# Attention and two wide layers on one core: where the 256-key bias slabs and the first weight unit stand in the start

## Chip, core and metric

The kernel runs on one core of a Trainium2 chip. The metric is the device time in microseconds (us). Three timed runs of the kernel before gave 657.86, 659.28 and 660.02 us, a median of 659.28 us. The profiled execution took 659.89 us in all, and the span from its first to its last instruction is 657.6 us; all times inside the trace are counted from the start of that span.

The engines are called as in the profile: PE (matrix multiply, with PEld for its weight loads), DVE (vector), ACT (scalar and activation), POOL (GpSimd), SP (here only the queue that issues transfers).

## What is computed

Attention with a local window, a few global keys and a distance bias, and behind it two wide layers with other nonlinearities:

```python
scores = scale * q @ k.T                       # B=2, H=8, S=768, D=64
keep   = is_global | is_local                  # 8 global keys, 96 local ones
bias   = -slopes[h] * dist                     # dist is the distance, n_local for far global keys
scores = where(keep, scores + bias, -1e9)
x = softmax(scores) @ v                        # as 1536 tokens x 512
h = x @ w_in;   x = (relu(h) + log1p(exp(-|h|))) @ w_out      # 512 -> 2048 -> 512
h = x @ w_in2;  x = (h * clip(h + 3, 0, 6) / 6) @ w_out2
```

## The kernel before

**Attention by quads.** Each batch of 768 rows is cut into 6 blocks of 128 rows, so that there are 12 blocks. A quad is one block and four heads, so there are 24 of them, two to a block, counted 0 to 23. A block sees its own keys and those of the block before it (256 keys), and the first block of a batch sees only its own (128 keys). For a quad, `att_s` makes the scores on PE (L481). Per head, DVE then adds the bias slab and takes the row's minimum of the negated scores (L487, called a minima instruction here), and ACT does the exponential with its row sum (L492). DVE adds a small constant to the row sums and takes the reciprocal (L377, L378, "rs"), and POOL scales the rows by it (L380). `att_t` transposes the scaled rows on PE (L513), ACT copies the result out (L515, "pT"), and `att_v` multiplies by the values (L531). Behind the second quad of a block ACT and DVE split the block's result into a high and a low part (L538, L539).

**Bias slabs.** The tile `bias` holds for each of the 8 heads three slabs of 128 keys. The slab for the own block of a first block (index 2) is made on ACT (L446, eight instructions). The slabs for 256 keys (indices 0 and 1) are made on DVE by `bias_of` (L449), one instruction for a head, from the mask tile `far` (L441 to L444). Quads 0 and 1 belong to the first block and need only L446. Quad 2 is the first that needs L449.

**Weights by units.** The weights come as 64-bit words in units of 512 KB. A unit is loaded (L121, on SP), its absolute value is taken on ACT (L140) and clamped on POOL (L143). DVE rebuilds its bits in three steps (L144, L147, L148), POOL rounds it to the high part (L103), and DVE subtracts to get the low part (L153). `weight_step(m)` puts m units into the program, with the loads of up to five units ahead of the one at hand. Both layers are made of such units; the first multiplication of the first layer (`hf`, from L201) needs units 0 and 1, the second one (`accf`) needs units 4 and 5.

**The start.** The lead at L616 to L628 makes 12 multiplications of zeros (`warm`, L614), then for p = 0 to 4 the scores of all quads up to p + 2, the values, more `warm`, the transposes and the units of `LEAD_UNITS`. Just ahead of quad 2's scores it makes one unit and all eight 256-key slabs. Behind the lead, `layers.run` mixes the remaining quads into the first layer: two quads into the first `hf` item, one into every later half.

**What sets the order.** PE's order is the program's, by `keep_in_program_order`. On the other engines a scheduler of the framework places the instructions, with the bias slabs held in program order. Every engine runs its own instructions strictly in the order in which they stand.

Of the kernel before, what the change touches and what calls it, by code (L numbers as in the profile page):

```python
# [12 lines left out]
ALU = mybir.AluOpType  # L13
# [4 lines left out]
B, H, S, D = 2, 8, 768, 64  # L18
# [14 lines left out]
LEAD_UNITS = (2, 1, 1, 1, 1)  # L33
# [6 lines left out]
SCALE = 0.125  # L40
# [342 lines left out]
def fast_path(tc, ident, nf, counts, q, k, qt, kt, v, weights, out, flag):  # L383


    with ExitStack() as ctx, ExitStack() as actx:
# [58 lines left out]
        for h in range(H):  # L445
            nc.scalar.mul(bias[:, h, 2, :], far[:, 2, :], -SLOPES[h] / SCALE)  # L446

        def bias_of(h):
            tc.keep_in_program_order(nc.vector.tensor_scalar(  # L449
                out=bias[:, h, 0:2, :], in0=far[:, 0:2, :], scalar1=-SLOPES[h] / SCALE, scalar2=None, op0=ALU.mult  # L450
            ))

        pms, pTs = {}, {}
        s_tags = [(ps_s, f"s{j}") for j in range(2)]
# [1 line left out]
        def att_s(k):  # L456

            n, e = divmod(k, KC // 2)
            i, slot = n % NB, n % 3
            if e == 0:  # L460
                if n + 1 < B * NB:
                    load_block(n + 1)
                load_values(n)
                if i == 0:
                    nc.vector.tensor_copy(gk, kT[:, :, slot, 0:MAX_GLOBAL])
            before = (n - 1) % 3
            w = P if i == 0 else 2 * P
            nsl = w // P
            mo = 2 if i == 0 else 0
            step = before - slot  # L470
            end = slot + nsl * step
            ks = slice(slot, min(end, 3) if end >= 0 else None, step)
            two = layers.acc_tags if k < LEAD and k % 2 else s_tags
            ps = [layers.bank(t, f"s{k}_{j}", (P, 2, 2, P)) for j, t in enumerate(two)]
            pm = ap_m.tile([P, 4, 2 * P], F32, tag="pm", name=f"pm{k}")
            nm = ap_m.tile([P, 4], F32, tag="nm", name=f"nm{k}")
            sm = ap_m.tile([P, 4], F32, tag="sm", name=f"sm{k}")
            for a in range(2):
                for j in range(2):
                    hp = slice(j * D, (j + 1) * D)  # L480
                    layers.ordered(lambda: nc.tensor.matmul(  # L481
                        ps[j][:, a, 0:nsl, :], lhsT=qT[n][hp, 2 * e + a, :], rhs=kT[hp, 2 * e + a, ks, :],
                        start=True, stop=True,
                    ))
            for z in range(4):
                pmz = pm[:, z, 0:w]
                nc.vector.tensor_tensor_reduce(  # L487
                    out=pmz, in0=ps[z % 2][:, z // 2, 0:nsl, :].rearrange("p s t -> p (s t)"),
                    in1=bias[:, 4 * e + z, mo:mo + nsl, :].rearrange("p s t -> p (s t)"),
                    scale=-SCALE, scalar=3.0e38, op0=ALU.add, op1=ALU.min, accum_out=nm[:, z:z + 1],  # L490
                )
                nc.scalar.activation(pmz, pmz, AF.Exp, bias=nm[:, z:z + 1], scale=-1.0, accum_out=sm[:, z:z + 1])  # L492
            rs = ap_m.tile([P, 4], F32, tag="rs", name=f"rs{k}")
            softmax_rows(nc, sm, rs, [pm[:, z, 0:w] for z in range(4)])
            if e == KC // 2 - 1 and 1 <= i < NB - 1:
                nc.vector.tensor_copy(kT[:, :, slot, 0:MAX_GLOBAL], gk)
            pms[k] = pm
# [118 lines left out]
        warm_up(WARM)  # L616
        for p in range(LEAD):
            while step["s"] < min(p + AHEAD, quads):
                if step["s"] == 2:
                    layers.weight_step(1)  # L620
                    for h in range(H):
                        bias_of(h)
                att_step("s")
            att_step("v", p - V_LAG + 1)
            warm_up(FILL[p])
            for _ in range(2):
                att_step("t")
            layers.weight_step(LEAD_UNITS[p] - (p == 0))  # L628
        layers.run(Att, check_step)


# [176 lines left out]
```

## Time and profile before

| quantity | value |
|---|---|
| median of three timed runs | 659.28 us |
| profiled execution, in all | 659.89 us |
| its span | 657.6 us |
| PE busy | 628.1 us (96% of the span) |
| DVE, ACT, POOL busy | 429.8, 375.4, 148.5 us |
| mean granted PE clock | 0.988 of full speed |

The share of busy time alone does not tell where time is lost: PE is nearly always busy behind the first 75 us, and has its holes ahead of them. So the table of stretches, the list of waits and the order of time of the first 75 us are what is to be read here.

### The profile page before, as it was taken

The numbers are of one execution on the slowest core, as the hardware profiler recorded it, in microseconds if no ns is written. First come the engines' busy times: TensorE is split into PE (matmuls) and PEld (weight loads), VectorE is DVE, ScalarE is ACT, GpSimd is POOL, SyncE is SP. The second block draws the span as 40 slices with busy tenths as digits, with TensorE's granted clock in tenths as the row PEclk, the third lists the DMA queues.
The fourth block names the chain that finished last, engine by engine and source line by source line (L and its number), as shares of the span: only waits on it lengthen the run. The fifth ranks groups of instructions, "written<-read, shape, count | busy, mean of one in ns | idle before, by whom it ended". The sixth has DMA issues, their size and how long they took to land.

```text
span 657.6 us, 9611 instructions
## 1 busy us (share of the span) xinstructions
PE 628.1 (96%) x3481; PEld 514.6 (78%) x3481; DVE 429.8 (65%) x902; ACT 375.4 (57%) x786; POOL 148.5 (23%) x192
## 2 busy tenths in 40 slices
PE   8587998999999999999999999999999999999995
PEld 4366887889999888877788888888877888888874
DVE  5897568654789999999998995225832333424242
ACT  5577778775587977867687852325675222212220
POOL 3575454531024132625200420000100000000000
PEclk9698999999999999999999999999999999999999
DMA  8452331101035233433311132000473000001011
GB/s 281 168 201 87 116 97 53 37 21 70 33 98 160 96 129 104 136 113 112 129 48 52 46 129 96 1 1 32 118 219 81 0 1 0 1 1 64 1 65 69
DMA packets 24937, 53.67 MB, mean 82 GB/s; under 512 B 2480, under 2 KB 8880, under 8 KB 24880
## 3 DMA queue, kind: packets, MB, share of 16 engines
q1 hardware_dynamic: 24880, 52.96, 24.8%
q8 instruction: 29, 0.48, 0.3%
q14 instruction: 28, 0.23, 0.1%
HBM read 49.81 MB, written 3.15 MB: 81 GB/s over the span
## 4 chain that ended last, share of the span: by engine, by line
PE 62%; DVE 19%; ACT 6%; DMA 4%; POOL 4%; issue 3%; SPq 0%; ACTq 0%; POOLq 0%; DVEq 0%
PE acc L201 22%; PE h L201 22%; PE accf L201 6%; PE hf L201 5%; DMA chk<-in_q 3%; DVE wa L147 2%; DVE wa L148 2%; POOL pm L380 2%; DVE w L153 2%; ACT pm L492 2%; PE ptp L513 2%; DVE pm L487 2%; PE s L481 2%; POOL wa L143 1%; DVE gl L193 1%
## 5 line engine op out<-in xcount | busy, mean ns | idle before, releaser
L201 PE MATMUL h<-xsh,w 128*128 128x512 f32 x624 | 170.3, 396 | 0.4 <-DVE t L187 0.4
L201 PEld LDWEIGHTS h<-xsh,w 128*128 128x128 f32 x624 | 116.7, 188 | 29.5 <-DVE t L187 1.6
L143 POOL TENSOR_SCALAR wa<-wa 128x512 f32<-128x512 f32 x56 | 76.3, 1368 | 240.2 <-ACT wa L140 239.9
L201 PE MATMUL acc<-w,gh 128*128 128x512 f32 x384 | 120.6, 395 | 0.0
L191 DVE SCALAR_TENSOR_TENSOR t<-t,h 128x512 f32<-128x512 f32 x48 | 32.9, 686 | 96.7 <-ACT t L190 96.7
L190 ACT ACTIVATE t<-h,three 128x512 f32<-128x512 f32 x48 | 33.0, 687 | 105.2 <-PE h L201 105.1
L201 PE MATMUL h<-xsl,w 128*128 128x512 f32 x312 | 87.8, 396 | 0.0
L193 DVE TENSOR_TENSOR gl<-t,gh 128x512 fp32r<-128x512 f32 x78 | 55.2, 708 | 47.3 <-ACT gh L192 47.0
L201 PEld LDWEIGHTS acc<-w,gh 128*128 128x128 f32 x384 | 72.0, 188 | 17.4
L201 PE MATMUL acc<-gh,w 128*128 128x512 f32 x240 | 78.9, 396 | 0.3 <-DVE part L297 0.2
L201 PE MATMUL acc<-w,gl 128*128 128x512 f32 x192 | 76.3, 397 | 0.8 <-ACT part L303 0.4
L192 ACT CAST gh<-t 128x512 fp32r<-128x512 f32 x78 | 48.3, 619 | 50.3 <-PE acc L201 24.3
L201 PEld LDWEIGHTS h<-xsl,w 128*128 128x128 f32 x312 | 58.5, 188 | 14.1
L380 POOL TENSOR_SCALAR pm<-pm,rs 128x256 f32<-128x256 f32 (+1 forms) x96 | 51.0, 549 | 44.5 <-DVE rs L378 33.2
L201 PE MATMUL accf<-ghf,w 128*128 128x256 f32 x288 | 59.6, 291 | 0.6 <-ACT ghf L192 0.6
L492 ACT ACTIVATE pm<-pm,nm 128x256 f32<-128x256 f32 (+1 forms) x96 | 46.0, 480 | 16.5 <-DVE nm L487 16.3
L201 PEld LDWEIGHTS acc<-gh,w 128*128 128x128 f32 x240 | 44.9, 188 | 11.9 <-DVE part L297 0.6
L201 PEld LDWEIGHTS accf<-ghf,w 128*128 128x128 f32 x288 | 47.3, 191 | 2.2 <-issue 1.2
L201 PE MATMUL acc<-gl,w 128*128 128x512 f32 x120 | 47.5, 396 | 0.0
L153 DVE TENSOR_TENSOR w<-wa,w 128x512 fp32r<-128x512 f32 x56 | 38.9, 696 | 9.2 <-ACT w L105 8.3
L201 PE MATMUL hf<-xsh,w 128*128 128x256 f32 x288 | 44.8, 286 | 0.0
L201 PEld LDWEIGHTS acc<-w,gl 128*128 128x128 f32 x192 | 36.0, 188 | 11.0 <-DVE gl L193 1.7
(105 smaller groups left out, 989.2 us busy)
## 6 DMA issues: line engine op xcount, KB each, us to landing
raw<-in_w2i SPq DMA_DIRECT2D x16, 512.0 KB, 3.3
raw<-in_w2o SPq DMA_DIRECT2D x16, 512.0 KB, 3.3
raw<-in_w1i SPq DMA_DIRECT2D x14, 512.0 KB, 3.6
raw<-in_w1o SPq DMA_DIRECT2D x12, 512.0 KB, 3.3
V<-in_v SPq DMA_DIRECT2D x12, 256.0 KB, 2.9
chk<-in_q SPq DMA_DIRECT2D x12, 256.0 KB, 3.3
chk<-in_k SPq DMA_DIRECT2D x12, 256.0 KB, 2.8
out_x<-part SPq DMA_DIRECT2D x12, 256.0 KB, 2.1
```

The costliest lines, as they stand in the source:

```text
L143: nc.gpsimd.tensor_scalar(out=a, in0=a, scalar1=W_HI, scalar2=W_LO, op0=ALU.min, op1=ALU.max)
L147: nc.vector.scalar_tensor_tensor(out=ai, in0=hi, scalar=-2 ** 30, in1=ai, op0=ALU.bitwise_and, op1=ALU.bitwise_or)
L148: nc.vector.scalar_tensor_tensor(out=ai, in0=lo, scalar=29, in1=ai, op0=ALU.logical_shift_right, op1=ALU.bitwise_or)
L153: nc.vector.tensor_tensor(out=wl, in0=a, in1=r32(wh), op=ALU.subtract)
L190: nc.scalar.activation(t1, hf, AF.Relu, bias=self.three[:, 0:1])
L191: nc.vector.scalar_tensor_tensor(out=t3, in0=t1, scalar=6.0, in1=hf, op0=ALU.min, op1=ALU.mult)
L192: nc.scalar.copy(gh, t3)
L193: nc.vector.tensor_tensor(out=gl, in0=t3, in1=r32(gh), op=ALU.subtract)
L201: return self.nc.tensor.matmul(out, lhsT=a, rhs=b, start=start and z == 0, stop=stop and z == len(seq) - 1, **kw)
L380: nc.gpsimd.tensor_scalar(out=t, in0=t, scalar1=rs[:, j:j + 1], scalar2=0.0, op0=ALU.mult, op1=ALU.add)
L481: layers.ordered(lambda: nc.tensor.matmul(ps[j][:, a, 0:nsl, :], lhsT=qT[n][hp, 2 * e + a, :], rhs=kT[hp, 2 * e + a, ks, :], start=True, s ...
L492: nc.scalar.activation(pmz, pmz, AF.Exp, bias=nm[:, z:z + 1], scale=-1.0, accum_out=sm[:, z:z + 1])
```

## The change

The eight slabs are no longer made ahead of quad 2. Four of them (heads 0 to 3) stand directly behind the masks, ahead of quad 0's minima; the other four stand inside `att_s` of quad 0, behind its minima. The one unit of weights that stood ahead of quad 2 goes, and p = 0 makes two units where it made one, so that the lead has six units as before.

```diff
-        def bias_of(h):
-            tc.keep_in_program_order(nc.vector.tensor_scalar(
-                out=bias[:, h, 0:2, :], in0=far[:, 0:2, :], scalar1=-SLOPES[h] / SCALE, scalar2=None, op0=ALU.mult
-            ))
+        def bias_of(hs):
+            for h in hs:
+                tc.keep_in_program_order(nc.vector.tensor_scalar(
+                    out=bias[:, h, 0:2, :], in0=far[:, 0:2, :], scalar1=-SLOPES[h] / SCALE, scalar2=None, op0=ALU.mult
+                ))
+
+        bias_of(range(H // 2))
...
                 nc.scalar.activation(pmz, pmz, AF.Exp, bias=nm[:, z:z + 1], scale=-1.0, accum_out=sm[:, z:z + 1])
+            if k == 0:
+                bias_of(range(H // 2, H))
...
             while step["s"] < min(p + AHEAD, quads):
-                if step["s"] == 2:
-                    layers.weight_step(1)
-                    for h in range(H):
-                        bias_of(h)
                 att_step("s")
...
-            layers.weight_step(LEAD_UNITS[p] - (p == 0))
+            layers.weight_step(LEAD_UNITS[p])
```

PE's order is the same in both. On the other engines the order differs from quad 0 to about quad 12 and is the same from there to the end of the path that is executed. Three places follow; the line numbers of the changed kernel are up to five higher (L490 is L487 of before, L450 is L449, L495 is L492, L520 is L515).

On DVE, behind the minima of quads 0 and 1. Before (`part_90` is the scratch tile of weight units 0 to 3, `w_0` to `w_3` are converted weights, `pm_269` is quad 2):

```order
L496 COPY kT<-gk 128x4x32
L144 TENSOR_SCALAR part_90<-part_90 128x512
L147 SCALAR_TENSOR_TENSOR part_90<-part_89,part_90 128x512
L148 SCALAR_TENSOR_TENSOR part_90<-part_89,part_90 128x512
...
L147 SCALAR_TENSOR_TENSOR part_90<-raw_0_237,part_90 128x512
L153 TENSOR_TENSOR w_0_244<-part_90,w_0_243 128x512
L449 TENSOR_SCALAR bias<-far 128x256 x8
L153 TENSOR_TENSOR w_1_309<-part_90,w_1_308 128x512
L148 SCALAR_TENSOR_TENSOR part_90<-raw_0_237,part_90 128x512
L487 ISA pm_269,nm_270<-s_0_267,bias 128x256
```

DVE, the same place and what leads up to it, in the changed kernel (`pm_193`, `pm_221`, `pm_250`, `pm_321` are quads 0 to 3, `rs_212` belongs to quad 0, `rs_336` to quad 3):

```order
L450 TENSOR_SCALAR bias<-far 128x256 x4
L490 ISA pm_193,nm_194<-s_0_191,bias 128x128
...
L450 TENSOR_SCALAR bias<-far 128x256 x4
L490 ISA pm_221,nm_222<-s_0_219,bias 128x128
...
L377 TENSOR_SCALAR rs_212<-sm_195 128x4
L490 ISA pm_250,nm_251<-s_0_248,bias 128x256
...
L378 RECIPROCAL rs_212<-rs_212 128x4
...
L490 ISA pm_321,nm_322<-s_0_319,bias 128x256
...
L378 RECIPROCAL rs_336<-rs_336 128x4
L144 TENSOR_SCALAR part_90<-part_90 128x512
```

The slabs and the minima of quads 2 and 3 moved ahead of the first unit's DVE work, which was most of three units ahead of quad 2 and is now mixed with the minima of quads 4 to 8.

On ACT, from quad 1's exponentials on. Before:

```order
L492 ACTIVATE pm_213,sm_215<-pm_213,nm_214 128x128 x4
L140 ACTIVATE part_90<-part_89 128x512
L515 COPY pT_0_298<-ptp_0_297 128x2x128
L515 COPY pT_1_303<-ptp_1_302 128x2x128
L140 ACTIVATE part_90<-part_89 128x512
L515 COPY pT_0_354<-ptp_0_353 128x2x128
L515 COPY pT_1_359<-ptp_1_358 128x2x128
L140 ACTIVATE part_90<-raw_0_237 128x512
L492 ACTIVATE pm_269,sm_271<-pm_269,nm_270 128x256 x4
```

ACT, the same place in the changed kernel (`pm_250` is quad 2, `pm_321` quad 3):

```order
L495 ACTIVATE pm_221,sm_223<-pm_221,nm_222 128x128 x4
L495 ACTIVATE pm_250,sm_252<-pm_250,nm_251 128x256 x4
L520 COPY pT_0_279<-ptp_0_278 128x2x128
L520 COPY pT_1_284<-ptp_1_283 128x2x128
L140 ACTIVATE part_90<-part_89 128x512 x2
L495 ACTIVATE pm_321,sm_323<-pm_321,nm_322 128x256 x4
```

Quad 2's exponentials moved ahead of the first units' L140; quad 3's stand behind the first two of them.

On DVE, ahead of the first `glf`, the low part that the first `accf` multiplies by. Before (`pm_814` is quad 10):

```order
L188 TENSOR_TENSOR t3f_699<-t3f_699,t2f_700 128x512
L153 TENSOR_TENSOR w_2_367<-part_90,w_2_366 128x512
L487 ISA pm_814,nm_815<-s_0_812,bias 128x256
...
L487 ISA pm_814,nm_815<-s_1_813,bias 128x256
...
L193 TENSOR_TENSOR glf_697<-t3f_699,ghf_696 128x512
```

DVE, the same place in the changed kernel:

```order
L153 TENSOR_TENSOR w_2_367<-part_90,w_2_366 128x512
L188 TENSOR_TENSOR t3f_699<-t3f_699,t2f_700 128x512
L490 ISA pm_814,nm_815<-s_0_812,bias 128x256
...
L193 TENSOR_TENSOR glf_697<-t3f_699,ghf_696 128x512
L490 ISA pm_814,nm_815<-s_1_813,bias 128x256
```

The low part now stands behind two minima of quad 10 instead of four, and the unit's last step stands one place earlier. On POOL the rounding (L103) that this L153 waits for stood behind a quad's four L380 and now stands ahead of them. On SP the transfers of the third block (`qT`, `kT`) and the values of the second stood behind the first five weight loads and now stand ahead of them.

## Rows read from the trace of the kernel before

**Rows 1.** The page, parts 1 and 2: busy time, and PE's granted clock.

```profile
PE 628.1 (96%) x3481; PEld 514.6 (78%) x3481; DVE 429.8 (65%) x902; ACT 375.4 (57%) x786; POOL 148.5 (23%) x192
PEclk9698999999999999999999999999999999999999
```

**Rows 2.** Table of stretches: start and end, length, busy us (instructions) by engine.

```profile
core 0: us, PE busy (x) PEld busy (x) DVE busy (x) ACT busy (x) POOL busy (x), PEclk, DMA share, GB/s
...
6.40:15.00 8.60, 8.23 (x59) 4.96 (x58) 4.27 (x23) 6.72 (x29) 3.99 (x10) 1.00 0.98 352
15.00:24.30 9.30, 0.12 (x3) 0.01 (x1) 9.16 (x25) 1.86 (x6) 2.94 (x4) 0.78 0.86 299
24.30:40.00 15.70, 14.82 (x115) 10.57 (x115) 13.23 (x59) 15.35 (x50) 10.37 (x21) 0.80 0.37 125
40.00:61.55 21.55, 15.97 (x147) 13.30 (x145) 17.26 (x55) 15.56 (x45) 15.59 (x23) 0.99 0.45 150
61.55:75.00 13.45, 13.39 (x116) 12.29 (x117) 8.13 (x30) 8.44 (x25) 6.19 (x10) 0.89 0.30 99
75.00:160.00 85.00, 81.23 (x744) 71.23 (x743) 55.53 (x177) 63.78 (x168) 35.07 (x63) 1.00 0.17 49
...
6.37:61.55 55.18, 39.18 (x318) 28.83 (x317) 43.92 (x158) 39.49 (x127) 32.88 (x57) 0.90 0.58 200
```

**Rows 3.** Waits of PE: total us, times, longest; from 0 to 75, then behind 75.

```profile
PE s L481 <- DVE nm L487: 9.2, 1, 9.2
PE accf L201 <- DVE glf L193: 3.1, 1, 3.1
...
PE ptp L513 <- ACT pT L515: 3.7, 9, 1.1
```

**Rows 4.** DVE in order of time (start, us), then line L147's own durations (min/median/max ns).

```profile
7.34 0.29 DVE L487 CUSTOM_DVE_ANT_0 pm<-s,bias 128x128 f32<-128x128 f32 x1 [0.97 <-ACT bias L446]
20.31 1.69 DVE L449 TENSOR_SCALAR bias<-far 128x256 bf16<-128x256 f32 x8
23.13 0.41 DVE L487 CUSTOM_DVE_ANT_0 pm<-s,bias 128x256 f32<-128x256 f32 x1
23.47 0.41 DVE L487 CUSTOM_DVE_ANT_0 pm<-s,bias 128x256 f32<-128x256 f32 x1
...
L147 DVE SCALAR_TENSOR_TENSOR part<-part,part x3: 687/691/978, 14.7 to 54.1; 128x512 int32<-128x512 int32 x3
```

**Rows 5.** ACT in order of time: first unit, then quad 2's first exponential.

```profile
11.42 0.67 ACT L140 ACTIVATE part<-part 128x512 f32<-128x512 f32 x1 [0.23 <-DMA part<-in_w1i]
...
23.59 0.51 ACT L492 ACTIVATE pm<-pm,nm 128x256 f32<-128x256 f32 x1 [7.44 <-DVE nm L487]
```

**Rows 6.** PE in order of time: scores of quads 4 and 5, the first `hf`.

```profile
24.29 2.42 PE L481 MATMUL s<-kT,qT 64*128 64x256 f32 x8 [9.18 <-DVE nm L487]
...
30.36 1.15 PE L481 MATMUL s<-kT,qT 64*128 64x256 f32 x8
...
39.97 0.62 PE L201 MATMUL hf<-xsh,w 128*128 128x256 f32 x3
```

**Rows 7.** POOL in order of time: row scaling of three quads, and of one.

```profile
27.03 5.47 POOL L380 TENSOR_SCALAR pm<-pm,rs 128x256 f32<-128x256 f32 x12 [3.12 <-DVE rs L378]
...
43.53 3.46 POOL L380 TENSOR_SCALAR pm<-pm,rs 128x256 f32<-128x256 f32 x4
```

**Rows 8.** Order of time ahead of the first `accf`: DVE, and one transfer of the chain.

```profile
50.63 0.42 DVE L487 CUSTOM_DVE_ANT_0 pm<-s,bias 128x256 f32<-128x256 f32 x1 [1.43 <-PE s L481]
50.66 3.15 DMA kT<-in_kt
...
58.88 0.69 DVE L153 TENSOR_TENSOR w<-part,w 128x512 fp32r<-128x512 f32 x1 [1.42 <-POOL w L103]
...
60.87 0.68 DVE L193 TENSOR_TENSOR glf<-t3f,ghf 128x512 fp32r<-128x512 f32 x1
```

**Rows 9.** Stretch behind the first `glf`: length, PE busy, granted clock, DMA.

```profile
62.00:66.00 4.00, 4.00 (x26) 0.68 0.10 28
```

## Prediction

> **What bounds the kernel now.** First the page: PE is busy 96% of the span, and its granted clock falls short of full only in the first slices [rows 1]. Then the table of stretches, for where PE's holes are: from 75 to 160 us PE is busy 81.2 of 85 us, and the longest entry of its waits behind 75 us is 3.7 us in nine pieces [rows 2, 3]. So from 75 us on PE is the bound, and since the order of every engine is the same there in both kernels, whatever is gained or lost ahead of that point should reach the end undiminished. Ahead of it PE has two large holes: 9.2 us before quad 4's scores, which wait for quad 2's minima on DVE, and 3.1 us for the first `glf` [rows 3]. Third the order of time around the first hole: from 15 to 24.3 us DVE is busy 9.16 of 9.3 us, nearly all of it with weight units and the eight slabs; ACT sits idle 7.44 us, POOL is busy 2.94 us [rows 2, 5]. Quad 2's first minima instruction comes at 23.13 us, right behind this work [rows 4].
>
> The tempting reading is that 9.2 us are to be had. But behind the hole PE is not the limit: from 24.3 to 40 us ACT is busy 15.35 of 15.7 us, and from 40 to 61.55 us DVE 17.26 of 21.55 us [rows 2]. The units' DVE work isn't removed, only put elsewhere. So I count on DVE, the engine with the most work up to the end of the first `glf` at 61.55 us (60.87 + 0.68 [rows 8]): from 6.37 us, the end of the masks, it is busy 43.92 of 55.18 us, so it idles 11.26 us [rows 2]. What can be gained there is that idle time, less what must stay.
>
> **The change part by part.**
>
> *Four slabs ahead of quad 0.* Eight cost 1.69 us, so four cost 0.85 us [rows 4]. DVE idles 0.97 us there for ACT's own slab, and this hides them; without that cover they would cost their 0.85.
>
> *Four slabs behind quad 0's minima.* These delay quad 1's minima by 0.85 us to an end at about 9.9 us. Quad 0's exponentials end at about 9.65 either way, since ACT makes its slabs first. So quad 0's row sums are taken up at 9.95, and by the new order two minima of quad 2 (0.345 us each, from the distance of the starts [rows 4]) stand ahead of the reciprocal. POOL starts quad 0's scaling about 1 us later than before, and so does PE its first transposes. That is the price at the front, paid once; PE's four `warm` multiplications and quad 3's scores move with it.
>
> *Quads 2 and 3 ahead of the units.* Quad 2's minima go from 23.13 to about 10.1 us, their exponentials (0.5 us each [rows 5]) on ACT to 11.2 to 13.2. DVE then waits in its order twice: for quad 2's row sums, from 12.05 to 13.2 (1.15 us), and for quad 3's. Quad 3's scores end near 14.1, but on ACT its exponentials stand behind two copies and two L140 of 0.67 us [rows 5], so they run from about 15.2 to 17.2, and DVE idles from 15.35 (1.85 us). From there I find, walking the new order with durations of before, no wait of DVE until quad 9: quad 4's scores stand ready at 17.5, quad 5's at 21.3, and ACT and PE wait for DVE. The first `hf` starts near 33 us.
>
> *SP.* Three transfers of 256 KB pass the five weight loads. At 352 GB/s in that stretch [rows 2] they delay the first units by 2.2 us; L140 waited 0.23 us for its data at 11.42 [rows 5], so the data are there at about 13.4. ACT comes to that L140 only at 13.85: hidden. Were the cover gone, each us would delay quad 3's exponentials by one.
>
> *Quad 9 and the globals.* DVE waited 1.43 us for quad 9's scores [rows 8]; by the walk it still waits 0.9. The copy of the next batch's global keys waits for a transfer of 3.15 us that starts when those scores end [rows 8]: 1.0 us by the walk, with more DVE work standing ahead of it now.
>
> *First `glf`.* The 1.42 us for POOL's rounding [rows 8] should go, since that rounding now stands ahead of a quad's scaling. Two of four minima leave the path: 0.69 us.
>
> *Sum on DVE.* Idle that stays: 0.12 + 1.15 + 1.85 + 0.9 + 1.0 = 5.0 us. End of the first `glf`: 6.37 + (43.92 - 0.69) + 5.0 = 54.6 us instead of 61.55, 6.95 us earlier.
>
> *Contention.* From 15 to 24.3 us the units' DVE work ran beside a POOL that was mostly idle; now it runs beside the row scaling. Where both meet, both stretch: L147 takes 0.69 or 0.98 us [rows 4], and four scalings take 1.82 us beside minima (a third of 5.47) but 3.46 us beside a unit [rows 7]. Nine such DVE instructions (L147, L148, L153 of three units) at 0.29 us more are 2.6 us at most; nothing at least, since some met POOL before. I take half, 1.3 us, and 0.8 us for handovers that the walk leaves out. That leaves 4.85 us.
>
> The Trainium skill, SBUF — State Buffer, section "Who interferes with whom", says that a DVE instruction with two SBUF inputs and a GpSimd instruction that reads SBUF share a port pair which the first one holds for its whole length. It speaks against this change, which brings such pairs together. The rows above show the stretch, though on DVE with 0.29 us less than a whole POOL instruction's length. Were each of the nine DVE instructions held for a whole scaling of 0.46 us (5.47 by 12), 4.1 us would stand where the sum has 1.3, and the gain would be 2.7 us.
>
> *Clock.* Behind the two holes the granted clock is lower: eight score multiplications take 2.42 us at 24.29, and 1.15 us at 30.36 [rows 6]. That first dip lies where other engines bind. The second, 0.68 from 62 to 66 us [rows 9], lies where PE binds: 64% of 4 us at half speed (1.2 instead of 2.4 GHz) costs 1.3 us. The hole ahead of it shrinks by the walk from 3.6 to about 1.5 us. I credit half, 0.65 us; bounds 0 and 1.3.
>
> Gain: 4.85 + 0.65 = 5.5 us. From the profiled execution's 659.89 us that is 654.4; the median lies 0.6 us lower and would give 653.8. I say 654.1. The bounds of the parts give a gain from about 3 to 8.3 us.
>
> **The rivals.**
>
> *Contention and order eat it.* DVE loses the full 2.6 us, POOL's scaling runs at 3.46 us per quad instead of 1.82 through quads 4 to 6 and holds the transposes for 2 of those 5 us: a gain of about 2 (1 to 3), 657.5 us. For it: POOL and DVE are both dense there now. Against: by the walk POOL has one to two us of slack in each quad. The port rule named above would lead here too.
>
> *The whole hole comes back.* If the units fit into DVE's idle time without a new wait, PE gets its 9.2 us and the dip's 1.3: 649.4 us. Against: this needs 9.2 of DVE's 11.26 idle us, and two waits of 3 us together stand in the new order.
>
> *Slower by the clock.* PE now runs through 18 to 55 us with many short holes in place of one long one. If these keep it at half speed, the 16 us of PE work from 40 to 61.55 [rows 2] become 32 in a stretch of 21.55, PE becomes the bound there, and some 10 us are lost against 5.5 gained: 664 us. It decides from about 11 us of half clock beyond today's. Against: with holes of up to 1.3 us in it, that stretch had 0.99 [rows 2].
>
> *The change does nothing.* The order of the built program shows quad 2's minima ahead of the units, so only a wait not foreseen (late data for the first L140) could undo it; it is in the first rival.
>
> **How the numbers follow.** Forecast (gain 3 to 8.3): 0.70. First rival: 0.15, half of it under 2 us. Whole hole: 0.08. Slower: 0.07. What this measurement can tell from no change is about 0.3%, 2 us. Faster by more: 0.70 + 0.07 + 0.08 = 0.85, set to 0.84; within: 0.09; slower: 0.07. The range runs from 650.5 (most of the whole hole left out) to 658.3 us (a gain of 1, the weak end of the first rival).
>
> **What would show it.** In the new trace: quad 2's minima near 10 us; no PE wait of 9 us; DVE idle for row sums near 12 and 15 us, and hardly from 18 to 40; the first `hf` at 33 to 35 us instead of 39.97 [rows 6], the first `glf` ending at 55 to 57, a clock of 0.9 or more behind it, and everything from 75 us on moved by one amount. It is wrong if the first L140 waits for data past 15 us, if L380 groups of 3 us line up ahead of PE's transposes, or if the gain at the first `glf` is not found at the end.

## The result, and the profile after

| quantity | before | after |
|---|---|---|
| median of four timed runs | 659.65 us (657.86 to 660.17) | 649.65 us (648.48 to 650.82) |
| profiled execution, in all | 659.89 us | 648.48 us |
| its span | 657.6 us | 646.3 us |
| mean granted PE clock | 0.988 | 0.997 |

The ratio is 0.985, with a 95% interval of 0.983 to 0.988. The kernel became 10.0 us faster where 5.5 were forecast, and the time lies 0.85 us under the low end of the range. The sign and the place were right; the size was too small by almost half. The profiled execution of after is the fastest of its four, so its 11.4 us against before show a little more than the medians do.

The table of stretches of the changed kernel (from:to in us, length, then busy time and count of PE, PEld, DVE, ACT, POOL, the granted clock, the DMA share and GB/s):

```profile
15.00:24.30 9.30, 8.72 (x71) 6.13 (x71) 8.24 (x33) 9.08 (x30) 6.89 (x13) 1.00 0.72 246
24.30:40.00 15.70, 11.96 (x109) 8.62 (x106) 15.70 (x47) 9.76 (x31) 14.57 (x20) 1.00 0.69 226
40.00:61.55 21.55, 17.96 (x162) 15.37 (x163) 18.93 (x56) 17.14 (x49) 15.86 (x22) 1.00 0.44 150
75.00:160.00 85.00, 81.18 (x737) 71.93 (x734) 54.95 (x166) 60.07 (x154) 32.60 (x56) 1.00 0.17 54
6.62:52.63 46.01, 37.75 (x316) 27.14 (x317) 41.66 (x153) 37.74 (x122) 35.40 (x55) 1.00 0.68 233
```

Against [rows 2], PE now works from 15 us on, the clock is at 1.00 in all of these stretches, and from 24.3 to 40 us DVE has no idle time at all: it is now the full engine there, as ACT nearly was before. The last line is the count on which the prediction's sum rests, from the end of the masks to the end of the first `glf`: 46.01 us where it was 55.18. Behind 75 us the two kernels do the same amount of work per time (81.18 against 81.2 us of PE in 85).

What PE waits for in the first 75 us of the changed kernel (what it was about to do, what it waited for, us in total, times, the longest):

```profile
PE ptp L518 <- ACT pT L520: 4.4, 4, 2.8
PE px L536 <- ACT wa L140: 1.8, 1, 1.8
PE ptp L518 <- POOL pm L380: 1.1, 3, 0.5
PE accf L201 <- DVE glf L193: 0.3, 1, 0.3
```

The 9.2 us for quad 2's minima and the 3.1 us for the first `glf` of [rows 3] are gone. In their place stand waits for copied and scaled rows, 5.5 us in seven pieces, the longest 2.8. The order of time on DVE and PE of the changed kernel (start, us):

```profile
6.62 0.90 DVE L450 TENSOR_SCALAR bias<-far 128x256 bf16<-128x256 f32 x4
8.40 0.89 DVE L450 TENSOR_SCALAR bias<-far 128x256 bf16<-128x256 f32 x4
10.13 0.42 DVE L490 CUSTOM_DVE_ANT_0 pm<-s,bias 128x256 f32<-128x256 f32 x1
13.40 0.29 DVE L377 TENSOR_SCALAR rs<-sm 128x4 f32<-128x4 f32 x1 [1.45 <-ACT pm L495]
17.03 0.17 DVE L377 TENSOR_SCALAR rs<-sm 128x4 f32<-128x4 f32 x1 [1.03 <-ACT pm L495]
47.68 0.23 DVE L468 COPY gk<-kT 128x128 f32<-128x128 f32 x1 [0.16 <-DMA kT<-in_kt]
51.94 0.69 DVE L193 TENSOR_TENSOR glf<-t3f,ghf 128x512 fp32r<-128x512 f32 x1
...
32.46 0.62 PE L201 MATMUL hf<-xsh,w 128*128 128x256 f32 x3
52.69 0.39 PE L201 MATMUL accf<-glf,w 128*128 128x256 f32 x1 [0.34 <-DVE glf L193]
```

Quad 2's minima start at 10.13 instead of 23.13 us, the first `hf` at 32.46 instead of 39.97 [rows 6], and the first `accf` that takes `glf` at 52.69 instead of 61.61 us. That is 8.92 us at the last point at which the start holds PE up. The later `glf` show what is gained behind it. The third and the last of the 18, before and then after:

```profile
80.12 0.69 DVE L193 TENSOR_TENSOR glf<-t3f,ghf 128x512 fp32r<-128x512 f32 x1
215.41 0.79 DVE L193 TENSOR_TENSOR glf<-t3f,ghf 128x512 fp32r<-128x512 f32 x1
```

```profile
70.69 0.69 DVE L193 TENSOR_TENSOR glf<-t3f,ghf 128x512 fp32r<-128x512 f32 x1
206.12 0.81 DVE L193 TENSOR_TENSOR glf<-t3f,ghf 128x512 fp32r<-128x512 f32 x1
```

The third comes 9.43 us earlier and the last 9.29 us. So some 0.5 us more were gained between the first and the third. The clock fits this: it was 0.68 from 62 to 66 us [rows 9] and is now 1.00. The two profiled spans differ by 11.3 us, so 2 us of these came behind 215 us, where the orders are the same. What made them isn't shown, and neither is what lifts the medians' gain from 9.3 to 10.0 us.

### The profile page after: what moved, and what is told of

It reads as the page before. It is cut to its first block, busy times and chain, and to the rows that moved or that the text cites. A ratio compares the mean times of both kernels' runs of the same rounds, so it can differ in the third digit from the quotient of the medians.

```text
span 646.3 us, 9610 instructions
## 1 busy us (share of the span) xinstructions
PE 625.1 (97%) x3480; PEld 512.0 (79%) x3481; DVE 429.2 (66%) x902; ACT 375.1 (58%) x786; POOL 149.2 (23%) x192
## 4 chain that ended last, share of the span: by engine, by line
PE 68%; DVE 20%; ACT 6%; issue 2%; POOL 2%; DMA 1%; SPq 0%; DVEq 0%; ACTq 0%
PE h L201 26%; PE acc L201 26%; PE accf L201 6%; PE hf L201 5%; ACT pm L495 3%; DVE wa L147 2%; DVE wa L148 2%; DVE w L153 2%; DVE pm L490 2%; PE ptp L518 2%; DVE gl L193 1%; DVE t L187 1%; DVE t L186 1%; POOL pm L380 1%; DVE part L297 1%
## 5 line engine op out<-in xcount | busy, mean ns | idle before, releaser
L143 POOL TENSOR_SCALAR wa<-wa 128x512 f32<-128x512 f32 x56 | 72.3, 1296 | 243.9 <-ACT wa L140 243.5
L201 PEld LDWEIGHTS acc<-w,gh 128*128 128x128 f32 x384 | 72.0, 188 | 17.5
L380 POOL TENSOR_SCALAR pm<-pm,rs 128x256 f32<-128x256 f32 (+1 forms) x96 | 54.0, 580 | 38.0 <-DVE rs L378 18.3
L495 ACT ACTIVATE pm<-pm,nm 128x256 f32<-128x256 f32 (+1 forms) x96 | 46.1, 482 | 9.7 <-DVE nm L490 7.7
L153 DVE TENSOR_TENSOR w<-wa,w 128x512 fp32r<-128x512 f32 x56 | 39.2, 702 | 9.6 <-ACT w L105 8.3
L140 ACT ACTIVATE wa<-raw 128x512 f32<-128x512 f32 x53 | 35.5, 674 | 13.8 <-DVE w L153 7.3
```

Of the source, the lines that this page charges most:

```text
L140: first = nc.scalar.activation(a, raw.bitcast(F32)[:, :, 1], AF.Abs)
L143: nc.gpsimd.tensor_scalar(out=a, in0=a, scalar1=W_HI, scalar2=W_LO, op0=ALU.min, op1=ALU.max)
L153: nc.vector.tensor_tensor(out=wl, in0=a, in1=r32(wh), op=ALU.subtract)
L201: return self.nc.tensor.matmul(out, lhsT=a, rhs=b, start=start and z == 0, stop=stop and z == len(seq) - 1, **kw)
L380: nc.gpsimd.tensor_scalar(out=t, in0=t, scalar1=rs[:, j:j + 1], scalar2=0.0, op0=ALU.mult, op1=ALU.add)
```

## The experiments

Each edit is given against the kernel that its paragraph names. A point to keep in mind: whenever an instruction is moved or taken out, the scheduler may place others anew on DVE, ACT and POOL, so a run can differ in more than its edit. That decided how the first eight runs had to be read.

The useful yardstick over all runs is the start of the first `accf` by `glf`: taking it from the time leaves 595 to 598 us in every kernel, among them the changed one (52.69 us, 649.65), run 1 (57.27, 654.89) and the one before (61.61, 659.65). It is a rough one: the start is that of one profiled execution, and the spread of 3 us is as large as most effects below.

### One part alone: runs 1 and 2

**Run 1**, after with the unit put back ahead of quad 2:

```diff
             while step["s"] < min(p + AHEAD, quads):
+                if step["s"] == 2:
+                    layers.weight_step(1)
                 att_step("s")
...
-            layers.weight_step(LEAD_UNITS[p])
+            layers.weight_step(LEAD_UNITS[p] - (p == 0))
```

> The slabs stand as in the changed kernel, the one unit of weights stays ahead of quad 2 as before. Theory A (the eight slabs, behind a unit on DVE, were what held quad 2): quad 2's first minima near 10 us, the first glf ends at 52 to 54 us, time 650 to 652 us. Rival B (the unit ahead of quad 2, with its five loads and its L140, holds quad 2 by itself): quad 2 late by several us, 655 us or more.

Measured: 654.89 us (654.05 to 655.71), ratio 0.994 [0.992, 0.995].

**Run 2**, before with only the unit taken away from there, so that the eight slabs stand ahead of quad 2 as they did:

```diff
                 if step["s"] == 2:
-                    layers.weight_step(1)
                     for h in range(H):
                         bias_of(h)
...
-            layers.weight_step(LEAD_UNITS[p] - (p == 0))
+            layers.weight_step(LEAD_UNITS[p])
```

> All eight slabs stand ahead of quad 2 as before, the unit ahead of it is gone. Theory A: the slabs follow quad 1's row sums at once, quad 2's minima start near 13.5 us and not at 10, the first glf ends 1 to 3 us later than in the changed kernel (53.5 to 55.5), time 651 to 653 us. Rival C (the slabs must be made in DVE's idle time ahead of quad 1, or the gain is lost): 655 us or more.

Measured: 650.08 us (649.33 to 651.09), ratio 0.987 [0.985, 0.989]. Its first `hf` starts at 32.72 us.

Read alone, the two say that the unit's place is nearly all of the gain and the slabs' place little of it. Run 1 does not fit that reading, though: its quad 2 minima come at 9.82 us and its first `hf` at 34.05, 1.6 us later than in the changed kernel. It loses the larger part of its time behind that, at the first `ghf` and `glf`:

```profile
49.48 3.10 POOL L380 TENSOR_SCALAR pm<-pm,rs 128x256 f32<-128x256 f32 x4 [1.04 <-DVE rs L378]
52.55 0.61 POOL L103 TENSOR_SCALAR w<-part 128x512 fp32r<-128x512 f32 x1
...
53.20 0.69 DVE L153 TENSOR_TENSOR w<-part,w 128x512 fp32r<-128x512 f32 x1 [1.19 <-POOL w L103]
53.80 1.10 DVE L188 TENSOR_TENSOR t3f<-t3f,t2f 128x512 f32<-128x512 f32 x1
...
55.61 0.38 PE L201 MATMUL accf<-ghf,w 128*128 128x256 f32 x1 [3.31 <-ACT ghf L192]
57.27 0.58 PE L201 MATMUL accf<-glf,w 128*128 128x256 f32 x1 [1.28 <-DVE glf L193]
```

The rounding (L103) of the seventh weight unit stands on POOL behind the four scalings of quad 9, 3.10 us of them. DVE, which has that unit's subtraction (L153) ahead of the first `t3f` (L188), waits for it, and PE waits 4.6 us in two pieces.

### The transfers: runs 5 and 6

**Run 5**, after with the five weight loads issued ahead of the third block's queries and keys again:

```diff
             while step["s"] < min(p + AHEAD, quads):
+                if step["s"] == 2:
+                    while layers.loaded < 5:
+                        layers.unit_load(layers.loaded)
+                        layers.loaded += 1
                 att_step("s")
```

> The changed kernel with one thing put back: the five weight loads are issued on SP ahead of the third block's qT and kT, as before; the unit's conversion stays behind quad 2. Theory F (what the change gains over the slabs alone is that the third block's keys no longer stand behind 2.5 MB of weights): PE waits 2 to 3 us for kT ahead of quad 4's scores, the first glf ends 2 to 4 us later than 52.63, time 652 to 655 us. Rival G (the order of DVE and ACT decides, the keys are early enough): within 0.8 us of the changed kernel's 649.65.

Measured: 651.25 us (650.09 to 651.48), ratio 0.987 [0.985, 0.989]: 1.6 us more than after by the medians, though the intervals overlap. PE waits 2.34 us at 17.99 for quad 4's keys:

```profile
17.99 1.13 PE L484 MATMUL s<-kT,qT 64*128 64x256 f32 x8 [2.34 <-DMA kT<-in_kt]
```

**Run 6**, run 1 with the opposite: the keys and values ahead of the unit's loads.

```diff
                 if step["s"] == 2:
+                    load_block(2)
+                    load_values(1)
                     layers.weight_step(1)
...
-            if e == 0:
+            if e == 0 and k != 2:
```

> The kernel of the first experiment (slabs early, the unit kept ahead of quad 2) with the third block's transfers issued ahead of the five weight loads. Theory F: no wait for kT, and the 654.9 us of the first experiment fall to 650 to 651.5. Rival G (the unit's L140 and DVE work ahead of quads 3 and 4 cost it): 653.5 or more.

Measured: 654.68 us (653.81 to 657.0), the same as run 1. So the order on SP may be worth up to 1.6 us in the changed kernel, but it isn't what run 1 loses: the wait for `ghf` is 3.43 us there as well.

### The later four slabs: runs 7 and 8

**Run 7**, after with the second four slabs behind quad 2's minima.

```diff
-            if k == 0:
+            if k == 2:
                 bias_of(range(H // 2, H))
```

> The changed kernel with the second four slabs behind quad 2's minima instead of quad 0's, in the 1.45 us in which DVE waits for quad 2's row sums. The prediction's step (the second four delay POOL's first scaling and PE's first transposes by about 1 us at the front): first transposes at 10.7 to 11 us instead of 11.62, the first glf 0.5 to 1 us earlier, time 649 us. Rival H (DVE's work up to the first glf decides, whatever stands first): the first glf within 0.4 us of 52.63, time within 0.5 us.

Measured: 653.17 us (652.29 to 654.35). The first `hf` starts at 31.99 us, the earliest of all, and yet the kernel is 3.5 us slower than after: PE again waits 3.40 us for `ghf` and 1.19 for `glf`, and the clock falls to 0.66 from 55 to 60 us.

**Run 8**, run 7 with the copy of the global keys into `kT` on ACT, because it stands ahead of the first `glf` on DVE.

```diff
-                nc.vector.tensor_copy(kT[:, :, slot, 0:MAX_GLOBAL], gk)
+                nc.scalar.copy(kT[:, :, slot, 0:MAX_GLOBAL], gk)
```

> As the one ahead of it, and the copies of the global keys into kT (four of them up to the first glf, 1.8 us on DVE) are made on ACT, which is busy 9.8 of 15.7 us from 24.3 to 40. Theory H (DVE's work decides): the first glf 1 to 1.8 us earlier than there, time 647.5 to 648.5 us. Rival I (ACT's row of exponentials is as tight in the first 24 us, busy 9.08 of 9.3): no gain, or up to 1 us slower.

Measured: 654.27 us (654.09 to 654.45): no gain. The wait moved from `ghf` (0.61 us) to `glf` (3.06).

After eight runs one thing told the good from the bad. In the changed kernel and runs 2 and 5 (649.65 to 651.25 us) POOL rounds the seventh unit ahead of quad 9's scalings. In the kernel before and runs 1, 6, 7 and 8 (653.2 us and more) it does so behind them. Run 3, told below, has the rounding first as well, but keeps the first hole; run 4, also below, has no scalings of quad 9. Before, and then in the changed kernel:

```profile
55.09 3.17 POOL L380 TENSOR_SCALAR pm<-pm,rs 128x256 f32<-128x256 f32 x4 [2.38 <-DVE rs L378]
58.24 0.61 POOL L103 TENSOR_SCALAR w<-part 128x512 fp32r<-128x512 f32 x1
```

```profile
48.66 1.07 POOL L103 TENSOR_SCALAR w<-part 128x512 fp32r<-128x512 f32 x1 [2.28 <-DVE rs L378]
49.71 3.27 POOL L380 TENSOR_SCALAR pm<-pm,rs 128x256 f32<-128x256 f32 x4
49.76 0.69 DVE L153 TENSOR_TENSOR w<-part,w 128x512 fp32r<-128x512 f32 x1
```

The scheduler chose the place; no edit named it. The next four runs change this one place and little else.

### One rounding on POOL: runs 9 to 12

In runs 9 to 11 quad 9's scalings are queued behind the last rounding that stands in the program ahead of them, which is the seventh unit's:

```diff
-            softmax_rows(nc, sm, rs, [pm[:, z, 0:w] for z in range(4)])
+            with tc.issue_after(layers.rounded.ins) if k == 9 else ExitStack():
+                softmax_rows(nc, sm, rs, [pm[:, z, 0:w] for z in range(4)])
```

POOL's order then differs from that of the base kernel by this swap, and in run 11 by one more rounding behind it. On DVE and ACT a few instructions near `glf` move by one or two places.

**Run 9** is run 1 with this.

> The kernel of run 1 (early slabs, unit kept ahead of quad 2), with one change in POOL's order: the rounding (L103) of the seventh weight unit now stands ahead of quad 9's four row scalings, as it does in the changed kernel, instead of behind them. Theory G (the second hole hangs on this one place): in run 1 DVE waited 1.19 us for that rounding and then took 1.10 us for the first t3f (L188); both go, the first glf ends near 55.3 instead of 57.1 us, PE's wait for ghf and glf falls from 4.6 to about 2.5 us, the dip behind it shrinks: 652.3 us (651.7 to 653.2). Rival R (the hole comes from what arrives late there, the global keys' transfer and the unit itself, whatever POOL does first): 654.3 us or more, glf after 56.7.

Measured: 651.7 us (649.18 to 654.7), ratio 0.987 [0.985, 0.989]: 3.2 us less than run 1. PE's wait for `ghf` and `glf` fell from 4.6 to 3.2 us; the clock from 55 to 60 us is 0.50.

**Run 10** is the kernel before with this.

> The kernel before, with the same one change in POOL's order. Theory G: DVE's wait of 1.42 us ahead of the first glf goes, the first glf ends near 60.1 instead of 61.55 us and the granted clock behind it rises above 0.68: 657.5 us (656.7 to 658.2) against about 659.3 of the kernel before. Rival R: within 0.5 us of the kernel before.

Measured: 657.83 us (655.93 to 659.25), ratio 0.9973 [0.9958, 0.9988] from 10 runs; the kernel before, measured beside it, had 659.5. DVE no longer waits there, and the first `accf` by `glf` starts at 60.65 instead of 61.61 us; the dip behind it stayed, with a clock of 0.66 from 60 to 65 us:

```profile
57.13 0.68 DVE L155 TENSOR_TENSOR w<-part,w 128x512 fp32r<-128x512 f32 x1
...
60.65 0.38 PE L203 MATMUL accf<-glf,w 128*128 128x256 f32 x1 [0.94 <-DVE glf L195]
```

**Run 11** is run 7 with this.

> The kernel of run 7 (second four slabs behind quad 2's minima; 653.2 us, with the earliest first hf of all, 31.99 us), with the same one change in POOL's order. Theory G: L188 ends 0.8 us earlier, glf about 1 us, less of a dip: 651.9 us (651 to 652.6). If the early hf counts in full once the second hole is gone, 650 us. Rival R: 652.9 or more.

Measured: 651.93 us (650.67 to 652.56), 1.2 us less than run 7. Its early `hf` is still not worth anything: PE waits 2.9 us for `ghf` and 0.5 for `glf`, and the clock from 55 to 60 us is 0.66 as in run 7.

**Run 12** is the changed kernel with the opposite: the seventh unit's rounding and subtraction are put into the program behind quad 9's scalings (`scaled` is the last of these, which `softmax_rows` now returns).

```diff
-        self.cast(wh, a)
-        nc.vector.tensor_tensor(out=wl, in0=a, in1=r32(wh), op=ALU.subtract)
+        def split():
+            self.cast(wh, a)
+            nc.vector.tensor_tensor(out=wl, in0=a, in1=r32(wh), op=ALU.subtract)
+        if x == 6 and self.room:
+            self.later = split
+        else:
+            split()
...
+            if k == 9:
+                with tc.issue_after(scaled.ins):
+                    layers.later()
```

> The changed kernel with the opposite change: the rounding of the seventh weight unit, and the subtraction behind it, are put behind quad 9's four row scalings, as in the kernel before. Theory G: DVE waits about 2 us for that rounding ahead of the first glf, which ends near 54.6 instead of 52.63 us; PE's wait there grows from 0.3 to 2 us or more and a dip of the clock may come back: 652 us (651.3 to 653.2) against 649.65. Rival R: within 0.6 us of 649.65.

Measured: 652.45 us (650.57 to 653.45), 2.8 us more than after. The wait is back, in the form that it had before [rows 8]:

```profile
50.81 2.52 POOL L387 TENSOR_SCALAR pm<-pm,rs 128x256 f32<-128x256 f32 x4 [3.48 <-DVE rs L385]
53.30 0.61 POOL L103 TENSOR_SCALAR w<-part 128x512 fp32r<-128x512 f32 x1
...
53.95 0.69 DVE L155 TENSOR_TENSOR w<-part,w 128x512 fp32r<-128x512 f32 x1 [1.42 <-POOL w L103]
...
56.40 0.39 PE L208 MATMUL accf<-glf,w 128*128 128x256 f32 x1 [1.86 <-DVE glf L200]
```

The median times of all four came out within 0.6 us of what this theory gave, and the rival (late data and the unit itself) missed all four. By the medians one rounding's place is worth 1.2 to 3.2 us. The intervals are clear of each other for runs 1 and 9, and run 10's is clear of no change; those of runs 7 and 11 and of after and run 12 overlap, so there it is the sign that agrees. What was expected of the clock did not come: the dips of runs 9 to 11 stayed, and run 12 has none (1.00 from 55 to 60 us). Run 12's first `accf` by `glf` comes 3.7 us later, of which 1.0 us is there at its first `hf` (33.45) already, ahead of the swap. The profiled executions of runs 9, 11 and 12 are the slowest of their four, so their stretches show the upper end.

With this place held equal (the rounding first), the parts of the change can be read at last:

| median in us (ratio) | unit kept ahead of quad 2 | unit gone from there |
|---|---|---|
| slabs ahead of quad 2 | 657.83 (0.997), run 10 | 650.08 (0.987), run 2 |
| slabs early | 651.7 (0.987), run 9 | 649.65 (0.985), after |

Either part alone takes most of the hole away: by the medians 6.1 us by the slabs, 7.75 by the unit, 8.2 by both. By the ratios the two single parts are equal; the kernel before, measured beside each group of runs, had medians of 658.9 to 660.66, so a difference of 1.6 us between two of these fields is not told by medians alone. The reason is in the order: both stood in front of the same minima on DVE, and with either of them gone the scheduler puts quad 2 ahead of the units' bulk. In run 1 its minima start at 9.82 us and the first L144 at 15.32, in run 2 at 13.79 and 16.67. What looked after runs 1 and 2 like "the unit is everything" was mostly the swap on POOL, which run 1 had and run 2 had not.

### The clock in the first hole: run 3

Before, with 36 more multiplications of zeros ahead of quad 4's scores, to keep PE busy through the first hole:

```diff
             while step["s"] < min(p + AHEAD, quads):
+                if step["s"] == 4:
+                    warm_up(36)
```

> The kernel before, with 36 more multiplications of zeros (about 7.8 us at full clock) ahead of quad 4's scores, so that PE runs through the 9.2 us hole. The prediction's step (the first dip of the clock lies where other engines bind): the granted clock from 24 to 31 us is near 1.0 instead of 0.54, and the time is that of before within 0.7 us. Rival D (the slow clock was part of the price of the hole): 1 to 2.5 us faster than before.

Measured: 659.71 us (659.42 to 661.39), ratio 1.0016 [1.0004, 1.0029].

```profile
24.00:31.00 7.00, 4.90 (x30) 2.91 (x32) 5.42 (x28) 6.54 (x26) 2.88 (x7) 0.98 0.21 75
31.00:36.00 5.00, 5.00 (x38) 3.55 (x34) 2.75 (x13) 4.29 (x13) 3.84 (x9) 0.68 0.34 107
...
40.00:45.00 5.00, 4.35 (x24) 3.10 (x24) 4.93 (x18) 5.00 (x17) 1.23 (x2) 0.60 0.43 140
```

The clock from 24 to 31 us rose from 0.54 to 0.98, and quad 5's scores still start at 30.38 us, where they started at 30.36 [rows 6]. So that dip cost nothing at that place, as the prediction said. The total is inconclusive, because the scheduler moved DVE's order behind quad 4 and other dips came from 31 us on: the first `hf` starts at 45.27 us, 5.3 later than before, and the first `accf` by `glf` at 64.10, 2.5 later, and still the time is the same.

### Contention: runs 4 and 13

**Run 4** is the changed kernel, and **run 13** the kernel before, without the row scaling (L380) of quads 2 to 9. Both leave out a part of the softmax; only what they tell of contention is used.

```diff
-            softmax_rows(nc, sm, rs, [pm[:, z, 0:w] for z in range(4)])
+            softmax_rows(nc, sm, rs, [pm[:, z, 0:w] for z in range(4)] if not 2 <= k <= 9 else [])
```

> The changed kernel without POOL's row scaling (L380) of quads 2 to 9: that part of the softmax is left out. The prediction's term (DVE loses 1.3 us to POOL): L147, L148 and L153 of the first units fall to 0.69 us each, DVE is busy 1.3 to 2.6 us less up to the first glf, which ends at 50 to 51.3 us instead of 52.63. Theory E (POOL pays, from its slack): DVE's busy time up to the first glf changes by under 0.7 us; what the glf gains comes from PE's shorter waits alone.

> The kernel before without the row scaling (L380) of quads 2 to 9; this leaves out a part of the softmax, so its time is read for the contention between POOL and DVE alone. In the changed kernel the same cut took 2.0 us off DVE's busy time up to the first glf (41.66 to 39.68 us). If the contention was as large before the change (then the 1.3 us that the prediction added for it were counted twice), DVE's busy time up to the end of the first glf falls from 43.92 to 42.4 us or less. If it is new, as the prediction had it, it falls by less than 0.7 us, to 43.2 or more. The time in all stays within 1.5 us of the kernel before in both.

Measured, one execution each: 649.57 and 656.44 us. The stretch from the end of the masks to the end of the first `glf`, run 4 and then run 13:

```profile
6.40:51.98 45.58, 39.12 (x318) 28.63 (x317) 39.68 (x153) 37.64 (x122) 14.37 (x25) 0.96 0.69 240
```

```profile
6.79:58.47 51.68, 37.43 (x306) 27.13 (x303) 41.73 (x154) 37.55 (x122) 13.88 (x25) 0.90 0.60 208
```

In the changed kernel the scaling costs DVE 41.66 - 39.68 = 2.0 us for the same 153 instructions. In the kernel before it is 43.92 - 41.73 = 2.2 us, of which 0.69 are two minima of quad 10 that stand behind the first `glf` in run 13, so 1.5 us. The contention that the change adds on DVE is thus about 0.5 us and not 1.3, and most of it was there before. Run 4 also shows that it hardly matters for the end: without 21 us of POOL work, the first `accf` by `glf` comes 0.56 us earlier and the time is the same. DVE's idle time grew from 4.35 to 5.90 us there, so most of the busy time saved came back as waits. Run 13 is 4.2 us below the kernel before that was measured beside it (660.66 us), but that is no proof of the opposite, for its seventh rounding had no scalings left to stand behind.

### POOL or DVE: runs 14 and 15

The rounding of units 5 and 6 (run 14, with the seventh held ahead of quad 9) or of units 4 to 7 (run 15, `x in (3, 4, 5, 6)`) goes from POOL to ACT, in the hope of a kernel that beats both:

```diff
-        self.cast(wh, a)
+        if self.room and x in (4, 5):
+            nc.scalar.copy(wh, a)
+        else:
+            self.cast(wh, a)
```

> The changed kernel with the rounding of the fifth and the sixth weight unit on ACT instead of POOL, and the seventh unit's rounding held ahead of quad 9's scalings as in the changed kernel. If DVE's own work sets the first glf, as its 15.70 busy of 15.70 us between 24.3 and 40 us say, taking 1.7 us off POOL gives only what POOL's lower contention leaves: first glf 0 to 0.5 us earlier, 649.4 us (648.5 to 650.2). If POOL's chain sets it (PE waits 2.84 us at 42.43 for quad 7's scaled and copied rows), 1 to 1.7 us earlier: 648.3 us.

> As the run before it, with the rounding of the fourth to the seventh unit on ACT, so that no rounding stands on POOL in either place ahead of the first glf. If DVE sets the first glf: 649.2 us (648 to 650.5). If POOL does: 647.8 us. If ACT, which then has 2.3 us more, becomes late with the copies and exponentials: 651 us or more.

Measured: 650.56 us (649.82 to 653.03), ratio 0.9845 [0.983, 0.986], and 651.66 us (651.1 to 653.55), ratio 0.9875 [0.986, 0.989]; the kernel before, measured beside them, had 660.66. Neither beats the changed kernel (0.985): run 14 can't be told from it, run 15 is no better. The first `accf` by `glf` did not come earlier in either, but at 55.28 and 54.57 us instead of 52.69, so the forecast of its place failed. That POOL sets the pace is ruled out by run 4 and not by these two: in run 14 DVE is as full from 24.3 to 40 us as it was, but so is POOL, with 14.56 us instead of 14.57:

```profile
24.30:40.00 15.70, 11.98 (x110) 8.64 (x106) 15.70 (x44) 10.39 (x31) 14.56 (x19) 1.00 0.71 223
```

## Why the prediction was too small

**Right.** What bounds the start, and that the hole's 9.2 us are not simply there to be had. Both groups of slabs cost nearly what was said (0.90 and 0.89 us where 0.85 was forecast), quad 2's minima came at 10.13 (10.1 forecast), the first `hf` at 32.46 (33), quad 4's scores in time for minima at 17.64 (17.5). DVE stands for row sums as foreseen, 1.45 and 1.03 us (1.15 and 1.85). The 8.9 us at the first `glf` arrive at the end. Everything behind 75 us moved by one amount, as forecast, up to 215 us (9.4 to 9.3) but not to the end of the profiled span (11.3). Also right was a step of one line, that the 1.42 us for POOL's rounding would go, read from the order of the built program. By the medians of runs 10 and 12 it is worth 1.7 to 2.8 us; it is the larger part of what run 1 lacked.

**Wrong: the count on DVE.** The sum put the end of the first `glf` at 54.6 us and, with contention and handovers, 2.1 us later, at 56.7. It was 52.63. The 4.07 us are made up of three terms:

- *Contention and handovers*, 1.3 + 0.8 = 2.1 us added. Neither showed: DVE's busy time, with all its contention in it, came out below the forecast without any. This is the largest mistake. The prediction took the 0.98 us of L147 [rows 4] for a stretch by row scaling that would come on top, in a stretch in which POOL was "mostly idle". In the kernel before it stood in that very stretch, beside POOL's work on the units:

```profile
14.66 0.69 DVE L147 SCALAR_TENSOR_TENSOR part<-part,part 128x512 int32<-128x512 int32 x1
15.38 0.69 DVE L148 SCALAR_TENSOR_TENSOR part<-part,part 128x512 int32<-128x512 int32 x1
16.23 0.65 POOL L143 TENSOR_SCALAR part<-part 128x512 f32<-128x512 f32 x1 [1.89 <-ACT part L140]
16.44 0.98 DVE L147 SCALAR_TENSOR_TENSOR part<-part,part 128x512 int32<-128x512 int32 x1
```

  Runs 4 and 13 put the growth by row scaling at 0.5 us.
- *Busy time*, 43.23 us forecast and 41.66 measured, 1.57 less. Of before and then of after, the same steps of the units in the two stretches (count, busy us, mean ns; the sixth L144 of before starts at 61.48 us, behind the first `glf`, and adds nothing to 43.92):

```profile
L144 DVE TENSOR_SCALAR part<-part 128x512 int32<-128x512 int32 x6 | 3.3, 558 | 0.0
L148 DVE SCALAR_TENSOR_TENSOR part<-part,part 128x512 int32<-128x512 int32 x3 | 2.4, 788 | 0.1
L153 DVE TENSOR_TENSOR w<-part,w 128x512 fp32r<-128x512 f32 x5 | 3.5, 708 | 1.4 <-POOL w L103 1.4
```

```profile
L144 DVE TENSOR_SCALAR part<-part 128x512 int32<-128x512 int32 x5 | 2.2, 433 | 0.0
L148 DVE SCALAR_TENSOR_TENSOR part<-part,part 128x512 int32<-128x512 int32 x3 | 2.0, 680 | 0.0
L153 DVE TENSOR_TENSOR w<-part,w 128x512 fp32r<-128x512 f32 x5 | 4.2, 834 | 0.0
```

  L144 and L148 got shorter, L153 longer. Counted one by one, the 152 instructions that both stretches share add up to about 52.6 us before and 52.4 after. So only some 0.2 us are shorter instructions; the rest, some 1.4 us, is that neighbours overlap more. Before, two steps of one unit, of which the second needs the first, start 0.72 us apart (14.66 and 15.38 above). Now steps of two units follow each other, 0.60 us apart at the same length:

```profile
20.73 0.68 DVE L148 SCALAR_TENSOR_TENSOR part<-part,part 128x512 int32<-128x512 int32 x1
21.33 0.68 DVE L147 SCALAR_TENSOR_TENSOR part<-part,part 128x512 int32<-128x512 int32 x1
```

- *Idle time*, 5.0 us forecast and 4.35 measured, less 0.25 for masks that ended later in this execution. The largest part is the copy of the global keys: 1.0 us forecast, 0.16 measured.

**The clock.** Credited with 0.65 of at most 1.3 us; the profiled pair shows some 0.5 us between the first and the third `glf`.

**The SP step** said that three transfers passing the weight loads only delay the weights. Run 5 shows the other side: had they not passed, PE would have waited 2.34 us for quad 4's keys, by the medians 1.6 us of the time. The walk used the new order, so the sum was right, but the step named only the cost and not what it spares.

**The rivals.** The time is that of the rival by which the whole hole comes back (649.4 us), which had 0.08. Its condition was that 9.2 of DVE's 11.26 idle us vanish. In fact idle time fell by 6.9 us, and 2.3 us of busy time went: 0.7 us are the two minima that moved behind the first `glf`, as forecast, and 1.6 us that DVE's work overlaps more or is shorter. So the number was hit by a road of which it knew three quarters. It deserved more: two of the deductions that separate it from the forecast, contention and handovers, had no row that fixed their size, and both were taken on the same side. The rule that speaks against the change, the Trainium skill's SBUF — State Buffer, section "Who interferes with whom", did not decide here: the estimate of a whole scaling lost by each of nine instructions put 4.1 us on DVE, and the runs show 0.5 us added and 2.0 us for all scaling of quads 2 to 9. POOL pays as well: in the stretch up to the first `glf`, its scaling of a 128x256 tile went from a mean of 591 to 688 ns.

**Left open.** Whether early slabs still bring something once the unit is gone (run 2 against after, 0.987 and 0.985 with intervals that overlap) isn't settled. What holds `ghf` and `glf` up by 3.2 us in run 9 and 3.4 in run 11, with the rounding first, isn't either. No run is free of the scheduler's own moves; 9, 10 and 12 have the fewest.

## What to carry to other kernels

When a scheduler places the work, an edit that undoes one part can change the order somewhere else, and its time is then that of both: compare the orders of two kernels before their times, and hold the odd place fixed before saying which part the gain is due to. A count of one engine's busy and idle time up to the last point that holds up the bound engine gives the size of a gain; a deduction for contention belongs in it only as far as the trace of before lacks that contention. It is not exact either: in run 4, 2.0 us less of busy time brought 0.56 us. A hole that needs two things together is nearly gone when either is removed, so the parts of such a change don't add up.

## What was not expected of the hardware

The length of one hole does not tell what the clock does behind it. PE stood still for 2.84 us ahead of 42.43 in the changed kernel, and for 2.48 us ahead of 19.22 in run 1, and the granted clock stayed at 1.00 behind both. Behind the holes of 3.3 and 3.4 us in runs 1 and 7 it fell to 0.60 and 0.66 in the five us from 55. But in run 14 two holes of only 1.2 and 0.9 us, for `ghf` and `glf` with one multiplication between them, were followed by 0.66 in the same five us, and in run 12 one of 1.9 us by 1.00.

One kernel of one order, run 9, gave 649.18 us at a mean clock of 0.997 and 654.7 us at 0.991. The clock's 0.6% would be 3.9 us of these 5.5; only the slower execution has a trace, so the cause of the spread is not shown.
